# A float32 attention and gated feed-forward kernel: high and low parts interleaved row by row, sums by four transfers, statistics and value stores moved

## The chip, the cores and the metric

The kernel runs on one core of a Trainium2 chip. The metric is the device time of one execution in microseconds (us). PE is TensorE, DVE is VectorE, ACT is ScalarE, POOL is GpSimd; SP (SyncE) does nothing here but issue DMA transfers. DRAM is the chip's memory, SBUF the memory that the engines work from, in 128 partitions (rows), and PSUM the banks that PE writes its products to.

## The reference

```python
def reference(A_x, A_wqkv, A_wo, B_x, B_w1, B_w3, B_w2):
    x = A_x                                   # 1 x 2048 x 512, float32
    xn = layernorm(x, eps=1e-5)
    qkv = xn @ wqkv                           # 32 heads of 16
    p = softmax(q @ k.T * 16 ** -0.5)         # per head, 2048 x 2048
    s = (p @ v) @ wo
    g = silu((silu(xn @ w1) * (xn @ w3)) @ w2)   # inner width 1792
    return x + s * g
```

## The kernel before

**Exact products.** Each float32 operand is split into a high part, rounded to the format in which PE multiplies at full speed, and a low part, the rest. A product is then three: low by high, high by low, high by high (`split3`, `three`).

**Heads.** A head has 16 columns, so the three products of a score fit into one matmul with a contraction of 48 rows: the keys tile `ks` holds, per head, 48 rows made of high and low parts, and the queries tile `qs` the matching ones; further rows of `qs` carry the negative maxima of the scores (`mh`, `ml`), against rows of ones in `ks`. Two heads lie at partitions 0 and 64. The parts are made in the prologue, four blocks of 512 tokens at a time, stored to the DRAM tensors `qk` (`keep_rows`, L625), and loaded back as rows of a head (`load_k`, `load_q`). The helper `rows_in` does this with two transfers for each head: a merged one that brings both parts, 32 rows (L396), and one that brings one of the parts again, 16 rows (L398). In `qk` all 128 rows of one part lie together, then those of the other, so the merged transfer's source is 2 by 16 by columns.

**Order.** The kernel works in 32 half pairs (16 pairs of heads, two halves of 1024 queries). For each, maxima of scores are found first (matmul L422, DVE reduction L424), then scores again (L710), exponentials on ACT (L713), and products with the values (L726), whose 17th column of ones gives the sums. The matmuls of the feed-forward part (L1026) are woven in between. The order is written by hand in `ORDER_OF_ISSUE`; a small time model in the kernel only decides when side work, DMA issues among it, is put into the program. Each engine works through its own list in order. Nearly all DMA is issued by SP, in one list.

**The prologue** (to about 110 us) is ordered by the table `plan`: each row names a block's keys ("k"), queries ("q") or a tile's values ("v"), the tiles that are normalised and transposed next, the number of maxima to be done early, the number of token pieces to be stored to `xt` (L632), and further steps. `spread` computes a tile's mean and variance on DVE (three instructions) and two small POOL instructions; `norm` applies them on ACT. Values are copied by ACT into `vrow` (L560) and stored to DRAM `v` by DMAs that ACT issues (L566).

**Taking out a half pair** (`take_out`): the product is copied from PSUM to `ot`; the four rows of sums are brought to a 128 x 16 tile `sums` by one transfer (L737), inverted, stored to DRAM `rd` (L741), broadcast to all rows of `rb` by one transfer (L743), and multiplied on POOL (L745). This is done for 29 of the 32 half pairs; the last three take another way.

Semaphores: a transfer waits at its issuer until the one that used the same of eight slots before it has landed, whichever engine issued that one.

Of the kernel before, what the change touches and what calls it, by code (L numbers as in the profile page):

```python
# [9 lines left out]
F32 = mybir.dt.float32  # L10
F32R = mybir.dt.float32r
# [6 lines left out]
P = 128  # L18
S, D, F = 2048, 512, 1792
H, DH = 32, 16  # L20
NP = H // 2
KC = D // P
NT = S // P
TB = 4
# [3 lines left out]
VW = DH + 1  # L28
# [118 lines left out]
def raw(ap):  # L147
    return ap.bitcast(F32)
# [3 lines left out]
def kernel(ctx: ExitStack, tc: tile.TileContext, x, wqkv, wo, w1, w3, w2, out):  # L152
    nc = tc.nc
# [5 lines left out]
    dram = ctx.enter_context(tc.tile_pool(name="dram", bufs=1, space=DRAM))  # L159
# [18 lines left out]
    def bank(v):  # L178
        return take(v)[1]
# [2 lines left out]


    xt_d = [[dram.tile([P, KC * 512], F32R, name=f"xt{b}{s}") for s in range(2)] for b in range(TB)]
    qk_d = [dram.tile([2, P, S], F32R, name=f"qk{b}") for b in range(8)]
    o_d = [[dram.tile([P, 2, 512], F32R, name=f"o{b}{t}") for t in range(TB)] for b in range(KC)]
    v_d = dram.tile([NT, P, H * VW], F32, name="v")
    g_d = [dram.tile([512, D], F32, name=f"g{b}") for b in range(TB)]
# [19 lines left out]
    def run(gen):  # L208
        for _ in gen:
            pass  # L210
# [105 lines left out]
    class Weights:  # L316
# [47 lines left out]
    wts = Weights()  # L364
# [24 lines left out]
    def load_v(g):  # L389
        nc.sync.dma_start(room_v(g), v_d[:, :, g * GH * VW:(g + 1) * GH * VW].rearrange("t p (h d) -> p t h d", h=GH))  # L390

    def rows_in(t, two, src, r, h, cols):

        both = raw(src)[:, r:r + DH, cols]
        at = 64 * h + two * DH
        nc.sync.dma_start(raw(t)[at:at + 2 * DH, cols], both)  # L396
        at = 64 * h + 2 * (1 - two) * DH
        nc.sync.dma_start(raw(t)[at:at + DH, cols], both[1 - two])  # L398

    def load_k(p, cols=slice(0, S)):  # L400
        for h in range(2):
            rows_in(ks[p % 2], 0, qk_d[4 + p // 4], (p % 4) * 32 + h * DH, h, cols)

    def load_q(p, half, c=None):
        for h in range(2):
            rows_in(qs[p % 2], 1, qk_d[p // 4], (p % 4) * 32 + h * DH, h, c or slice(half * 1024, (half + 1) * 1024))

    def part_of(rbk, s):

        return raw(qk_d[rbk])[s if rbk < KC else 1 - s]  # L410

    mp, landed = {}, {}

# [38 lines left out]
    with tc.tile_pool(name="pro", bufs=1) as pro, tc.tile_pool(name="pros", bufs=1) as pros:  # L452
# [39 lines left out]
        def spread(t):  # L492

            st = pro.tile([P, 6], F32, tag="st", name="st", bufs=3)
            nc.vector.bn_stats(st, xin[t])
            mv = pro.tile([P, 2], F32, tag="mv", name="mv", bufs=6)
            nc.vector.bn_aggr(mv, st)
            ve = pro.tile([P, 1], F32, tag="ve", name="ve", bufs=3)
            nc.vector.tensor_scalar_add(ve, mv[:, 1:2], EPS)
            rs = pro.tile([P, 1], F32, tag="rs", name="rs", bufs=6)  # L500
            nc.gpsimd.tensor_tensor(rs, ve, minus, op=ALU.pow)
            nb = None
            if t > 0:
                nb = pro.tile([P, 1], F32, tag="nb", name="nb", bufs=6)
# [38 lines left out]
        def token_values(b, i):  # L543
            hi, lo = xts[b]
            ps = bank("m")
            three = [(h, k) for k in range(KC) for h in range(3)]
            if b == i == 0:

                three.sort(key=lambda e: ((2, 0, 1).index(e[0]), e[1]))
            elif b == 0:  # L550

                three.sort(key=lambda e: (e[0] == 0, e[1]))
            for n, (h, k) in enumerate(three):
                lhs = (lo, hi, hi)[h][:, k, i * P:(i + 1) * P]
                nc.tensor.matmul(ps, lhs, wv[k][h == 1], start=n == 0, stop=n == len(three) - 1)  # L555
# [4 lines left out]
            nc.scalar.copy(vrow[t % 4][:, :, 0:DH], v)  # L560
            nc.scalar.copy(vt[0][:, t, :, 0:DH], v[:, 0:GH, :])
            if b:
                store_values(t)

        def store_values(t):
            nc.scalar.dma_start(v_d[t], vrow[t % 4].rearrange("p h d -> p (h d)"))  # L566

        nc.gpsimd.memset(raw(ks[0]), 1.0)
        blank = iter([(raw(t), 0.0) for t in qs] + [(raw(ks[1]), 1.0)])
        spread(0)  # L570
        norm(0)
        split_w(0)
# [4 lines left out]
        split_w(2)  # L577
        split_w(3, nc.gpsimd)
        norm(1)
        vrow = [pros.tile([P, H, VW], F32, name=f"vrow{i}") for i in range(4)]  # L580
# [48 lines left out]
        def keep_tokens(n):  # L629
            for _ in range(n):  # L630
                b, s, k = next(stored_tokens)
                nc.sync.dma_start(raw(xt_d[b][s])[:, k * 512:(k + 1) * 512], raw(xts[b][s])[:, k, :])  # L632

        def more_tokens(n):

            transposed(n, xn.pop(n))
            if n + 2 < NT:
                norm(n + 2)
            if n + 4 < NT:
                spread(n + 4)  # L640

        def cols(b):
            return slice(b * 512, (b + 1) * 512)
# [1 line left out]
        def keys_here(b):  # L645
            return lambda: keep_rows(b, 1), lambda: load_k(0, cols(b))
# [8 lines left out]
            wts.pump(KC)  # L655
            wts.fill()

        def values_first():
            for t in range(TB):
                store_values(t)  # L660

        plan = [
            ("k", 0, (4, 5), 0, 0, keys_here(0)),
            ("q", 0, (6,), 0, 0, (values_first,)),
            ("v", 0, (7,), 0, 0, queries_here(0)),
            ("v", 1, (8,), 0, 1, ()),
            ("k", 1, (9, 10), 0, 2, ()),
            ("q", 1, (11,), 4, 2, keys_here(1)),
            ("v", 2, (12, 13), 5, 2, queries_here(1)),
# [4 lines left out]
            ("k", 3, (), 6, 1, (lambda: load_q(1, 0),)),  # L674
            ("q", 3, (), 6, 2, keys_here(3)),
            ("v", 1, (), 5, 2, queries_here(3) + (lambda: load_q(0, 1),)),
            ("v", 2, (), 6, 2, (blank_next, wts.start)),
# [4 lines left out]
            ("v", 3, (), 0, 0, ()),  # L682
        ]
        done = 0
        for what, n, tiles_, maxima_, pieces_, then in plan:
            if what == "v":
                run(token_values(1 + done // TB, n))
                done += 1
            else:
                token_rows(n, int(what == "k"))  # L690
            for _ in range(maxima_):
                max_unit(*next(early))
            for t in tiles_:
                more_tokens(t)
            for e in then:
                e()
            keep_tokens(pieces_)

    ring = ctx.enter_context(tc.tile_pool(name="ring", bufs=1))
# [29 lines left out]
    def take_out(p, half):  # L729

        ot = work.tile([P, 512], F32, tag="ot", name="ot", bufs=2)
        nc.scalar.copy(ot, pv)
        yield
        sums = work.tile([P, 16], F32, tag="sums", name="sums", bufs=2)
        rec = work.tile([P, 16], F32, tag="rec", name="rec", bufs=2)
        rd = dram.tile([4, 512], F32, name=f"rd{p * 2 + half}")
        nc.sync.dma_start(sums, ot[DH:P:32, :])  # L737
# [5 lines left out]
        nc.sync.dma_start(rb, rd.rearrange("j (o c) -> j o c", o=1).to_broadcast([4, 32, 512]))  # L743
# [307 lines left out]
    ov, wos, side, sums, there = {}, [], {}, {}, {}  # L1051
# [230 lines left out]
    for g in range(KC - 1):  # L1282
        p = 4 * g + 3
# [147 lines left out]
    for c in ORDER_OF_ISSUE:  # L1431
# [19 lines left out]
        elif c != "R":  # L1451
            what = (c.lower(), int(c.isupper()))
# [14 lines left out]
    ot, oh, ol = pt_tile(F32), pt_tile(F32R), pt_tile(F32R)  # L1467
# [20 lines left out]
    for t in range(4):  # L1488
        i, ps = take("o")
# [30 lines left out]
```

## Time and profile before

| | |
|---|---|
| Median of 3 runs | 1735.78 us (1734.87 to 1738.62) |
| Profiled execution | 1731.0 us, of which the span from first to last instruction 1729.2 |
| PE busy | 1698.3 us (98%) |
| DVE, ACT, POOL busy | 79%, 71%, 51% |
| Mean granted clock of PE | 0.995 |
| DMA moved | 184.81 MB, mean 107 GB/s |
| Merged loads (L396), 16-row loads (L398) | 104 each |

The profile's rows name a line, an engine, an operation and tiles as output<-input, with buffer numbers left out. "DMA ks<-qk" is a transfer's way from its issue to its landing, "SPq" is SP's time of issuing. In the chain of waits each row is a start and a length; in the timeline, the idle time before an instruction stands in brackets, with the name of what ended it by the profile. In windows, the last three columns are granted clock of PE (1.00 is full), busy share of the 16 DMA engines, and GB/s. A wait for several things is named after the last of them by the profile, so a name can be wrong where that engine had long been done.

### The profile page before, as it was taken

Reading aid. Unit: us, or ns where it says so; the run is one execution under the profiler, and the core shown is the slowest. Engines: PE = TensorE matmul, PEld = TensorE weight load, DVE = VectorE, ACT = ScalarE, POOL = GpSimd, SP = SyncE. Lnnn points to the kernel's source line nnn. Section 1 sums busy time; section 2 is a strip of 40 time slices with the busy share of each in tenths; the row PEclk is TensorE's granted clock in tenths of the full one; section 3 lists DMA queues with packets and bytes.
Section 4 is the critical chain, followed back from the end, with each engine's and each line's share of the span. In section 5 each row is a group of like instructions: output and inputs, shape, how many; then the busy total and the mean of one; then the engine's idle time right before and its main releaser. Section 6 shows DMA issues by size and latency. Waiting matters only on the chain.

```text
span 1729.2 us, 35378 instructions
## 1 busy us (share of the span) xinstructions
PE 1698.3 (98%) x13476; PEld 1128.3 (65%) x13476; DVE 1370.7 (79%) x2288; ACT 1230.9 (71%) x2449; POOL 878.9 (51%) x925
## 2 busy tenths in 40 slices
PE   9889999999998999999999999999999999999998
PEld 7566676666665767656666666766676666665466
DVE  5768988887886878788888778887887887888735
ACT  5237777778675777777777777777787777777852
POOL 5545553466544664366546663566456715753001
PEclk9989999999999999999999999999999999999999
DMA  6563433333234334142244424232332312331254
GB/s 230 190 205 113 134 106 86 96 112 93 78 112 133 107 102 120 56 109 54 72 131 141 132 83 128 75 90 60 98 100 75 81 38 71 92 108 35 77 176 175
DMA packets 164897, 184.81 MB, mean 107 GB/s; under 512 B 35640, under 2 KB 107320, under 8 KB 162520
## 3 DMA queue, kind: packets, MB, share of 16 engines
q1 hardware_dynamic: 161528, 176.52, 34.8%
q10 hardware_dynamic: 3200, 6.04, 0.9%
q8 instruction: 106, 1.74, 0.4%
q14 instruction: 63, 0.52, 0.1%
HBM read 135.36 MB, written 46.11 MB: 105 GB/s over the span
## 4 chain that ended last, share of the span: by engine, by line
PE 89%; DMA 5%; issue 2%; SPq 1%; POOL 1%; DVE 1%; ACT 1%; ACTq 0%; POOLq 0%; DVEq 0%
PE f L1026 31%; PE pv L726 26%; PE m L422 15%; PE e L710 15%; PE m L555 1%; DMA ks<-qk 1%; DMA qk<-sl 1%; DMA qs<-qk 1%; SPq L396 1%; DMA inh<-in_A_x_dram 1%; PE o L201 0%; PE m L437 0%; DMA ovh<-o 0%; PE o L203 0%; PE o L205 0%
## 5 line engine op out<-in xcount | busy, mean ns | idle before, releaser
L424 DVE TENSOR_REDUCE mp<-m 128x1 f32<-128x512 f32 x2048 | 1277.2, 683 | 242.9 <-PE m L422 170.9
L713 ACT ACTIVATE pt<-e 128x512 f32<-128x512 f32 x2048 | 1058.6, 611 | 270.9 <-PE m L422 134.4
L422 PE MATMUL m<-ks,qs 62*128 62x512 f32 x2048 | 744.7, 413 | 19.8 <-ACT g L849 8.2
L710 PE MATMUL e<-qs,ks 64*128 64x512 f32 x2048 | 742.2, 407 | 1.3 <-DMA qs<-ml 1.3
L726 PE MATMUL pv<-pt,vt 128*17 128x512 f32 x4096 | 480.1, 596 | 0.0
L422 PEld LDWEIGHTS m<-ks,qs 62*128 62x128 f32 x2048 | 352.0, 185 | 130.3 <-issue 38.2
L710 PEld LDWEIGHTS e<-qs,ks 64*128 64x128 f32 x2048 | 352.2, 184 | 105.9 <-issue 35.4
L726 PEld LDWEIGHTS pv<-pt,vt 128*17 128x17 f32 x4096 | 100.8, 97 | 253.9 <-issue 249.3
L1026 PE MATMUL f<-xtl,wh 64*128 64x512 f32 x504 | 184.0, 391 | 0.0
L1026 PE MATMUL f<-xth,wh 64*128 64x512 f32 x504 | 181.3, 392 | 0.0
L1026 PE MATMUL f<-xth,wl 64*128 64x512 f32 x504 | 181.1, 392 | 0.0
L1026 PE MATMUL f<-wh,hs 64*128 64x512 f32 x528 | 167.1, 393 | 0.0
L1026 PE MATMUL f<-xtl,xeh 64*128 64x512 f32 x440 | 161.0, 391 | 0.0
L1026 PE MATMUL f<-xth,xeh 64*128 64x512 f32 x440 | 158.4, 392 | 0.0
L1026 PE MATMUL f<-xth,xel 64*128 64x512 f32 x440 | 157.5, 395 | 0.0
L869 POOL TENSOR_TENSOR h<-g,h 128x512 f32<-128x512 f32 x56 | 72.1, 1288 | 163.1 <-ACT h L865 163.0
L340 POOL TENSOR_TENSOR wl<-wr,wh 128x512 fp32r<-128x512 f32 x105 | 135.5, 1290 | 8.8
L1026 PE MATMUL f<-xeh,hs 64*128 64x512 f32 x368 | 118.7, 394 | 0.4 <-POOL hs L871 0.4
L340 POOL TENSOR_TENSOR xel<-wr,xeh 128x512 fp32r<-128x512 f32 x87 | 112.3, 1290 | 7.3
L339 POOL TENSOR_SCALAR xeh<-wr 128x512 fp32r<-128x512 f32 x87 | 54.1, 621 | 120.3 <-PE m L422 56.1
L1026 PE MATMUL f<-wl,hs 64*128 64x512 f32 x264 | 99.0, 392 | 0.0
L339 POOL TENSOR_SCALAR wh<-wr 128x512 fp32r<-128x512 f32 x105 | 65.3, 622 | 63.6 <-PE e L710 42.1
(242 smaller groups left out, 2166.6 us busy)
## 6 DMA issues: line engine op xcount, KB each, us to landing
wr<-in_B_w_dram SPq DMA_DIRECT2D x168, 256.0 KB
ovh<-xt SPq DMA_DIRECT2D x36, 256.0 KB
ovl<-xt SPq DMA_DIRECT2D x36, 256.0 KB
qs<-qk SPq DMA_DIRECT2D x62, 128.0 KB
wr<-in_A_wqkv_dram SPq DMA_DIRECT2D x30, 256.0 KB
ks<-qk SPq DMA_DIRECT2D x30, 256.0 KB
o<-o SPq DMA_DIRECT2D x120, 64.0 KB
rb<-rd SPq DMA_DIRECT2D x29, 256.0 KB
```

Of the source, the lines that this page charges most:

```text
L339: nc.gpsimd.tensor_scalar(hi, t, 1.0, 1.0, op0=ALU.mult, op1=ALU.mult)
L340: nc.gpsimd.tensor_sub(lo, t, raw(hi))
L396: nc.sync.dma_start(raw(t)[at:at + 2 * DH, cols], both)
L422: nc.tensor.matmul(ps, qs[p % 2][64 * h:64 * h + KM, q0:q0 + P], ks[p % 2][64 * h:64 * h + KM, c * 512:(c + 1) * 512], start=True, stop=True)
L424: nc.vector.reduce_max(mp[p, half][:, h, qt, c:c + 1], ps, axis=AX.X)
L555: nc.tensor.matmul(ps, lhs, wv[k][h == 1], start=n == 0, stop=n == len(three) - 1)
L710: nc.tensor.matmul(ps, ks[p % 2][64 * h:64 * h + KR, k * P:(k + 1) * P], qs[p % 2][64 * h:64 * h + KR, q0:q0 + 512], start=True, stop=True)
L713: done = nc.scalar.activation(pt, ps, AF.Exp, scale=DH ** -0.5)
L726: nc.tensor.matmul(pv[32 * j:32 * j + VW, :], vt[2 * p // GH][:, key, 2 * p % GH + j % 2, :], pt, start=key < 2 if last else k == 0, stop= ...
L869: nc.gpsimd.tensor_mul(h2, g, h2)
L1026: nc.tensor.matmul(ps, left[r], right[r], start=starts and lane == 0, stop=ends and lane == 1)
```

## The change

1. `qk` in DRAM becomes rows by parts: the high and the low part of a row lie next to each other. The merged transfer is then 32 rows of one stride; rows of `ks` and `qs` interleave the parts, and the third sixteen rows repeat the high part for both.
2. The one transfer of sums becomes four, one for each row of sums; the one broadcast becomes four of 16 rows each, to the rows that hold products. The rows of `rb` between are set to 1 once.
3. Statistics of tiles 8 to 15 are computed two tiles at a time beside tiles 4 to 7 of the transposes; before, one tile beside each of tiles 4 to 11. Their small tiles get a buffer each.
4. Value stores go from ACT's list to SP's and are gathered: `keep_values(n)` stores what has been made until n remain. `vrow` has six buffers instead of four. Token pieces are spread a little differently over the plan.

```diff
-    qk_d = [dram.tile([2, P, S], F32R, name=f"qk{b}") for b in range(8)]
+    qk_d = [dram.tile([P, 2, S], F32R, name=f"qk{b}") for b in range(8)]
...
-        both = raw(src)[:, r:r + DH, cols]
-        at = 64 * h + two * DH
-        nc.sync.dma_start(raw(t)[at:at + 2 * DH, cols], both)
-        at = 64 * h + 2 * (1 - two) * DH
-        nc.sync.dma_start(raw(t)[at:at + DH, cols], both[1 - two])
+        both = raw(src)[r:r + DH, :, cols]
+        nc.sync.dma_start(raw(t)[64 * h:64 * h + 2 * DH, cols], both.rearrange("r s c -> (r s) c"))
+        nc.sync.dma_start(raw(t)[64 * h + 2 * DH:64 * h + 3 * DH, cols], both[:, high, :])
...
-        return raw(qk_d[rbk])[s if rbk < KC else 1 - s]
+        return raw(qk_d[rbk])[:, s if rbk < KC else 1 - s, :]
...
-            nc.scalar.copy(vrow[t % 4][:, :, 0:DH], v)
+            nc.scalar.copy(vrow[t % 6][:, :, 0:DH], v)
             nc.scalar.copy(vt[0][:, t, :, 0:DH], v[:, 0:GH, :])
-            if b:
-                store_values(t)
-
-        def store_values(t):
-            nc.scalar.dma_start(v_d[t], vrow[t % 4].rearrange("p h d -> p (h d)"))
+            made_values.append(t)
+
+        made_values = []
+
+        def keep_values(left):
+            while len(made_values) > left:
+                t = made_values.pop(0)
+                nc.sync.dma_start(v_d[t], vrow[t % 6].rearrange("p h d -> p (h d)"))
...
-        blank = iter([(raw(t), 0.0) for t in qs] + [(raw(ks[1]), 1.0)])
+        blank = iter([(raw(t), 0.0) for t in qs] + [(r, 1.0) for r in (raw(ks[1]), rb)])
...
-            if n + 4 < NT:
-                spread(n + 4)
+            for i in range(2 * n, min(2 * n + 2, NT)):
+                spread(i)
...
-            ("q", 0, (6,), 0, 0, (values_first,)),
+            ("q", 0, (6,), 0, 0, ()),
             ("v", 0, (7,), 0, 0, queries_here(0)),
-            ("v", 1, (8,), 0, 1, ()),
+            ("v", 1, (8,), 0, 0, ()),
...
+            if done > 1:
+                keep_values(int(what == "v"))
             keep_tokens(pieces_)
...
-        nc.sync.dma_start(sums, ot[DH:P:32, :])
+        for j in range(4):
+            nc.sync.dma_start(sums[32 * j:32 * j + 32, :], ot[32 * j + DH:32 * j + VW, :])
...
-        nc.sync.dma_start(rb, rd.rearrange("j (o c) -> j o c", o=1).to_broadcast([4, 32, 512]))
+        for j in range(4):
+            nc.sync.dma_start(rb[32 * j:32 * j + DH, :], rd[j:j + 1, :].to_broadcast([DH, 512]))
```

What moves in the lists: PE's list is the same in both, instruction by instruction. On SP in the prologue, from the loads of the first block's queries to the loads of the second block's keys, there stood before (`sh` and `sl` are the high and low part on their way to `qk`, `xt00<-xeh` a piece of tokens):

```order
L396 DMA qs0_108<-qk0_74 32x1x512
L398 DMA qs0_108<-qk0_74 16x512
L632 DMA xt00_66<-xeh_214 128x512 x3
L625 DMA qk4_78<-sh_615 128x512
L625 DMA qk4_78<-sl_616 128x512
L396 DMA ks0_110<-qk4_78 32x1x512
L398 DMA ks0_110<-qk4_78 16x512
```

and there stands now, lines being numbered a little differently (L395 is the merged load, L396 the 16-row one):

```order
L395 DMA qs0_108<-qk0_74 32x512
L396 DMA qs0_108<-qk0_74 16x512
L567 DMA v_98<-vrow0_235 128x544
L567 DMA v_98<-vrow1_236 128x544
L567 DMA v_98<-vrow2_237 128x544
L567 DMA v_98<-vrow3_238 128x544
L567 DMA v_98<-vrow4_239 128x544
L567 DMA v_98<-vrow5_240 128x544
L633 DMA xt00_66<-xeh_214 128x512 x2
L626 DMA qk4_78<-sh_647 128x512
L626 DMA qk4_78<-sl_648 128x512
L395 DMA ks0_110<-qk4_78 32x512
```

Six value stores have come in between, and one piece of tokens has moved behind the keys. On ACT, these stores stood before ahead of the copy of the next values and the high part of the next tile (`xth`):

```order
L616 COPY sc_498<-e_483 128x512
L526 CAST xth_437<-m_502 128x4x128
L514 ACTIVATE xn_509<-xin8_273,nb_456,rs_454 128x512
L566 DMA v_98<-vrow0_235 128x544
L566 DMA v_98<-vrow1_236 128x544
L566 DMA v_98<-vrow2_237 128x544
L566 DMA v_98<-vrow3_238 128x544
L560 COPY vrow0_235<-m_525 128x32x16
L561 COPY vt_243<-m_525 128x4x16
L566 DMA v_98<-vrow0_235 128x544
L526 CAST xth_437<-m_541 128x4x128
```

and now ACT's list runs through:

```order
L617 COPY sc_522<-e_507 128x512
L524 CAST xth_441<-m_526 128x4x128
L512 ACTIVATE xn_533<-xin8_277,nb_460,rs_458 128x512
L558 COPY vrow4_239<-m_555 128x32x16
L559 COPY vt_247<-m_555 128x4x16
L524 CAST xth_441<-m_570 128x4x128
```

On DVE, between one low part (`xtl`) and the next, there stand now the statistics of two tiles, where there was one:

```order
L525 TENSOR_TENSOR xtl_442<-m_472,xth_441 128x4x128
L493 BN_STATS st_481<-xin10_327 128x6
L495 BN_AGGR mv_483<-st_481 128x2
L497 TENSOR_SCALAR ve_485<-mv_483 128x1
L493 BN_STATS st_491<-xin11_329 128x6
L495 BN_AGGR mv_493<-st_491 128x2
L497 TENSOR_SCALAR ve_495<-mv_493 128x1
L525 TENSOR_TENSOR xtl_442<-m_526,xth_441 128x4x128
```

The small POOL steps of these statistics have moved with them, ahead of the splits of the next keys and queries.

More of the change, by code (lines that the diff above doesn't have):

```diff
@@ L390, in load_v, with rows_in @@
         nc.sync.dma_start(room_v(g), v_d[:, :, g * GH * VW:(g + 1) * GH * VW].rearrange("t p (h d) -> p t h d", h=GH))
-    def rows_in(t, two, src, r, h, cols):
-        both = raw(src)[:, r:r + DH, cols]
-        at = 64 * h + two * DH
-        nc.sync.dma_start(raw(t)[at:at + 2 * DH, cols], both)
-        at = 64 * h + 2 * (1 - two) * DH
-        nc.sync.dma_start(raw(t)[at:at + DH, cols], both[1 - two])
+    def rows_in(t, high, src, r, h, cols):
+        both = raw(src)[r:r + DH, :, cols]
+        nc.sync.dma_start(raw(t)[64 * h:64 * h + 2 * DH, cols], both.rearrange("r s c -> (r s) c"))
+        nc.sync.dma_start(raw(t)[64 * h + 2 * DH:64 * h + 3 * DH, cols], both[:, high, :])
     def load_k(p, cols=slice(0, S)):
         for h in range(2):
-            rows_in(ks[p % 2], 0, qk_d[4 + p // 4], (p % 4) * 32 + h * DH, h, cols)
+            rows_in(ks[p % 2], 1, qk_d[4 + p // 4], (p % 4) * 32 + h * DH, h, cols)
     def load_q(p, half, c=None):
         for h in range(2):
-            rows_in(qs[p % 2], 1, qk_d[p // 4], (p % 4) * 32 + h * DH, h, c or slice(half * 1024, (half + 1) * 1024))
+            rows_in(qs[p % 2], 0, qk_d[p // 4], (p % 4) * 32 + h * DH, h, c or slice(half * 1024, (half + 1) * 1024))
     def part_of(rbk, s):
-        return raw(qk_d[rbk])[s if rbk < KC else 1 - s]
+        return raw(qk_d[rbk])[:, s if rbk < KC else 1 - s, :]
     mp, landed = {}, {}
@@ L495, in spread @@
             nc.vector.bn_stats(st, xin[t])
-            mv = pro.tile([P, 2], F32, tag="mv", name="mv", bufs=6)
+            mv = pro.tile([P, 2], F32, tag="mv", name="mv", bufs=NT)
             nc.vector.bn_aggr(mv, st)
@@ L499, in spread @@
             nc.vector.tensor_scalar_add(ve, mv[:, 1:2], EPS)
-            rs = pro.tile([P, 1], F32, tag="rs", name="rs", bufs=6)
+            rs = pro.tile([P, 1], F32, tag="rs", name="rs", bufs=NT)
             nc.gpsimd.tensor_tensor(rs, ve, minus, op=ALU.pow)
@@ L503, in spread @@
             if t > 0:
-                nb = pro.tile([P, 1], F32, tag="nb", name="nb", bufs=6)
+                nb = pro.tile([P, 1], F32, tag="nb", name="nb", bufs=NT)
                 nc.gpsimd.tensor_scalar(nb, mv[:, 0:1], rs, -1.0, op0=ALU.mult, op1=ALU.mult)
@@ L579 @@
         norm(1)
-        vrow = [pros.tile([P, H, VW], F32, name=f"vrow{i}") for i in range(4)]
+        vrow = [pros.tile([P, H, VW], F32, name=f"vrow{i}") for i in range(6)]
         for v in vrow:
@@ L656, in weights_first @@
             wts.fill()
-        def values_first():
-            for t in range(TB):
-                store_values(t)
         plan = [
             ("k", 0, (4, 5), 0, 0, keys_here(0)),
-            ("q", 0, (6,), 0, 0, (values_first,)),
+            ("q", 0, (6,), 0, 0, ()),
             ("v", 0, (7,), 0, 0, queries_here(0)),
-            ("v", 1, (8,), 0, 1, ()),
+            ("v", 1, (8,), 0, 0, ()),
             ("k", 1, (9, 10), 0, 2, ()),
@@ L673 @@
             ("v", 0, (), 6, 2, (blank_next,)),
-            ("k", 3, (), 6, 1, (lambda: load_q(1, 0),)),
+            ("k", 3, (), 6, 2, (lambda: load_q(1, 0),)),
             ("q", 3, (), 6, 2, keys_here(3)),
             ("v", 1, (), 5, 2, queries_here(3) + (lambda: load_q(0, 1),)),
-            ("v", 2, (), 6, 2, (blank_next, wts.start)),
+            ("v", 2, (), 6, 2, (blank_next, blank_next, wts.start)),
             ("v", 3, (), 6, 2, (weights_first,)),
@@ L681 @@
             ("v", 2, (), 0, 0, ()),
-            ("v", 3, (), 0, 0, ()),
+            ("v", 3, (), 0, 0, (lambda: keep_values(0),)),
         ]
```

## The prediction

> **What bounds the kernel now.** I read the page first, then who PE waits for, then the chain of waits around each of those waits, then DMA by the microsecond.
>
> ```profile
> span 1729.2 us, 35378 instructions
> PE 1698.3 (98%) x13476; PEld 1128.3 (65%) x13476; DVE 1370.7 (79%) x2288; ACT 1230.9 (71%) x2449; POOL 878.9 (51%) x925
> ```
>
> PE is the bound: 31 us of the span are not PE work. The change leaves PE's list in the same order, so it can only win or lose waits, and what the clock does after them. Two answers on PE's waits, one for 0 to 125 us and one for 150 to 1700 us (total, times, longest):
>
> ```profile
> PE m L422 <- DMA ks<-qk: 6.7, 2, 5.5
> PE e L710 <- DMA qs<-ml: 1.3, 1, 1.3
> ...
> PE m L422 <- ACT g L849: 8.2, 3, 5.6
> PE m L422 <- DMA ks<-qk: 0.9, 1, 0.9
> ```
>
> Nearly all stand around a load of keys or queries. The timeline places them (start, length, in brackets the idle time before), and the chain tells what ran meanwhile (start, length):
>
> ```profile
> 46.56 0.73 PE L422 MATMUL m<-ks,qs 62*128 62x512 f32 x4
> 49.48 0.47 PE L422 MATMUL m<-ks,qs 62*128 62x512 f32 x1 [2.19 <-DVE mp L424]
> ...
> 60.51 0.50 PE L422 MATMUL m<-ks,qs 62*128 62x512 f32 x2 [1.87 <-DMA qs<-qk]
> 89.10 0.76 PE L422 MATMUL m<-ks,qs 62*128 62x512 f32 x1 [5.54 <-DMA ks<-qk]
> 90.97 1.62 PE L422 MATMUL m<-ks,qs 62*128 62x512 f32 x5 [1.11 <-DMA ks<-qk]
> ...
> 538.14 0.79 PE L422 MATMUL m<-ks,qs 62*128 62x512 f32 x1 [5.57 <-ACT g L849]
> ```
>
> ```profile
> 26.42 2.44 DMA qk<-sl
> ...
> 42.27 3.17 DMA qk<-sl
> 45.49 3.67 DMA ks<-qk
> 68.70 3.08 DVE mp L424 x5
> 77.63 7.26 DMA qk<-sl
> 86.72 4.11 DMA ks<-qk
> 92.59 4.71 PE m L555 x12
> 98.20 2.96 PE m L555 x12
> 108.26 4.01 DMA qs<-ml
> ...
> 516.55 7.57 SPq L396
> 524.99 9.80 DMA qs<-qk
> ```
>
> The reader is to see: a 256 KB store lands in 2.44 us in a quiet moment and in up to 7.26 us elsewhere; a 64 KB load takes 3.67 us; one load at 525 us takes 9.80 us after SP had hung 7.57 us on issuing another. The wait at 49.48 is named after DVE, but keys of block 1 landed at 45.49 + 3.67 = 49.16, and these are what that product first needs: I count it as a wait for keys. The one at 538.14 is the same at one remove: SP was late, so a store from a buffer that ACT wanted back was late. Why are the transfers slow? DMA share and GB/s are the last two columns:
>
> ```profile
> 44.00:45.00 1.00, 1.00 (x6) 0.82 (x5) 1.00 (x3) 1.00 (x2) 0.90 (x3) 1.00 0.13 49
> 50.00:51.00 1.00, 1.00 (x9) 1.00 (x10) 0.68 (x1) 0.43 (x1) 0.00 (x0) 1.00 1.04 385
> 520.00:521.00 1.00, 1.00 (x14) 0.52 (x8) 0.17 (x2) 0.04 (x1) 0.92 (x3) 1.00 0.12 49
> ```
>
> DMA can do 385 GB/s, yet right when PE is about to starve it does 49, on 0.12 of sixteen engines: two of them. What is under way then is the merged load of L396, whose source has the two parts, high and low, as its first dimension. Everything that lies behind it on those two engines is late too, a 128-row store for instance, since it has a share on each.
>
> The Trainium skill (DMA: Bandwidth & Descriptors, "Why a DMA increments its semaphore by 16 and not by 1") says that a transfer is given the largest number of engines up to 16 that divides the slowest dimension above 1 of both sides. By that rule the old merged load gets 2 engines and the new one, with 32 rows first, 16; the trace agrees for the old one (0.12 of 16).
>
> **The change part by part.**
>
> *Merged loads.* 32 rows of one stride instead of 2 by 16. Bounds for the new landing: above, today's 3.67 us; below, the 2.44 us of the quiet 256 KB store, which moves more bytes with 128 rows. I take the lower one: the load of one head pair and block, 192 KB, is 0.5 us at 385 GB/s. SP also issues it faster, if it becomes like its 16-row neighbour (ns, min/median/max):
>
> ```profile
> L396 SPq DMA_DIRECT2D qs<-qk x66: 600/622/7572, 37.0 to 1520.1; - x66
> L398 SPq DMA_DIRECT2D qs<-qk x66: 302/410/1161, 37.7 to 1525.3; - x66
> L737 SPq DMA_DIRECT2D sums<-ot x29: 594/611/2935, 169.3 to 1562.5; - x29
> L743 SPq DMA_DIRECT2D rb<-rd x29: 552/592/605, 192.3 to 1576.0; - x29
> ```
>
> That is 0.21 us for each of 104 (66 of queries, 38 of keys).
>
> *Value stores and statistics.* Today ACT issues the stores, and hangs while their slots come free (the name after the idle 4.59 us is that of a keys load, but the four instructions ahead of it are stores):
>
> ```profile
> 33.73 0.59 ACT L560 COPY vrow<-m 128x512 f32<-128x512 f32 x1 [4.59 <-DMA ks<-qk]
> 35.36 0.49 PE L201 MATMUL e<-xth,wkl 128*128 128x512 f32 x1 [1.12 <-ACT xth L526]
> 36.08 0.50 PE L203 MATMUL e<-xtl,wkh 128*128 128x512 f32 x1 [0.23 <-DVE xtl L527]
> ```
>
> Without that ACT is free at 33.73 - 4.59 = 29.1, and PE's two waits, 1.35 us, go. Statistics of two tiles instead of one now stand between two low parts on DVE; they cost what these rows say, and POOL has two more small steps ahead of its next split:
>
> ```profile
> 25.44 0.68 DVE L495 BATCH_NORM_STATS2 st<-xin 128x6 f32<-128x512 f32 x1
> 26.52 0.68 DVE L527 TENSOR_TENSOR xtl<-m,xth 128x512 fp32r<-128x512 f32 x1
> ```
>
> 26.52 - 25.44 = 1.08 us a tile on DVE. From 25.44 on, three low parts (0.6 each) and six tiles end by about 33.8, when PE (35.36 less its 1.12, 34.2) wants the last low part: covered, by 0.4 us. If that cover fails, PE loses a few tenths.
>
> What moves to SP is dearer: six stores of 272 KB plus two of 256 KB now lie, on SP's one queue, between the queries' load and the store of keys block 1. With that store (512 KB) they are 2.7 MB, 7.0 us at 385 GB/s.
>
> ```profile
> 38.80 0.41 SPq L398 DMA_DIRECT2D qs<-qk  x1
> ```
>
> The queries' last load was issued by 38.80 + 0.41 = 39.2; I have it at 37.7 (two merged loads of keys and two of queries, 0.21 less each, and some 0.7 for slots that come free sooner, an estimate). So data flows from about 38.2 to 45.2, has landed at 45.8 (today 45.44); the first head's two loads are issued by 46.7, and by 2 us of landing, a little under the quiet 2.44, its keys are there near 48.7. PE arrives at 47.29 - 1.35 = 45.9 and waits 2.8 us instead of 2.19. It goes on at 48.7 instead of 49.48: **0.8 us won** (bounds: 3.5 if all 1.35 + 2.19 went; -5 if the queue ran at the mean 211 GB/s of the next row instead of 385).
>
> ```profile
> 40.00:50.00 10.00, 7.81 (x38) 5.21 (x37) 9.48 (x21) 4.52 (x9) 6.44 (x11) 1.00 0.58 211
> 84.00:100.00 16.00, 9.79 (x32) 6.71 (x33) 6.00 (x10) 0.99 (x4) 0.00 (x0) 0.68 0.51 164
> 530.00:560.00 30.00, 24.43 (x181) 12.63 (x180) 16.11 (x29) 13.94 (x29) 16.71 (x18) 0.89 0.59 153
> ```
>
> *Queries block 1.* The keys' loads are issued by 47.6; two token stores and the queries' store, 1 MB, are then 2.7 us of queue and landed at 51.5, the load by 55. PE gets there at 60.5 - 49.5 = 11 us after the keys today, 1.9 of them idle, so at 48.7 + 9.1 = 57.8. **1.9 us won** (0 to 1.9).
>
> *Keys block 3.* By the same steps the keys of block 2 are issued near 61.5. Between them and this store lie 3.7 MB (four pairs of tokens, the queries' store, two values, next queries), 10 us of queue, then its own 512 KB: landed at 74, loaded at 77.5. PE is there at 89.10 - 5.54 - 2.7 = 80.9. Margin 3.4 us. So 5.54 + 1.11 go, and with them the slow clock: the mean of 0.68 over 84 to 100 us is (1 - 0.68)/0.5 x 16 = 10.2 us at half clock, in which twelve products took 4.71 instead of 2.96 us, five 1.62 instead of about 0.8 (four took 0.73 at 46.56), one some 0.3 more: 2.8 us. **9.45 us won** (0 to 9.45). Late next is DVE, with six maxima of 3.08/5 = 0.62 us, 3.7 us, for PE's twelve products and six maxima, 2.96 + 0.9 us: just fast enough.
>
> *First rows of maxima.* Their load took 4.01 us behind value stores; with 2.44 it would be early. But SP's half stands behind the last token and value stores. **1.0 us won** (0 to 1.3).
>
> *Main loop.* The wait at 538.14 and its clock: 0.89 over 530 to 560 is (1 - 0.89)/0.5 x 30 = 6.6 us at half clock, which would be 3.3 us lost had PE worked all through; it stood still for part of it, and I take 2.6; 5.57 + 2.6 = **8.2 us won** (0 to 8.2). The 0.9 us for keys at 924 us goes too: **0.9 us**. The other 2.6 us named after ACT I leave.
>
> *Sums and broadcast in four.* Four transfers of about 0.41 us for one of 0.61, and four for one of 0.59: 3.28 - 1.20 = 2.1 us more on SP in each of 29 half pairs, 60 us; the merged loads give back 104 x 0.21 = 22 us. SP does this beside PE, as it waits for others most of the time:
>
> ```profile
> SPq L449 <- ACT mh L440: 199.1, 31, 18.1
> ```
>
> The broadcast brings half the bytes, and rows of rb that are no longer brought are set once, 0.5 us on POOL. I take 0 (bounds: +1.3 and -10; see below).
>
> Sum: 0.8 + 1.9 + 9.45 + 1.0 + 8.2 + 0.9 = 22.3 us. The profiled execution took 1731.0 us (span 1729.2), 4.8 below the median of the runs, 1735.8. Its successor should take 1708.7, and the median be 1735.8 - 22.3 = **1713.5 us**.
>
> **The rivals.**
>
> *The value stores starve keys block 1.* At 211 GB/s the 2.7 MB take 12.8 us, PE waits 8.6 instead of 2.8 and the clock falls, as it did in both long waits: 5.8 + 2.7 less: 1722. For it: that mean was real in just this stage. Against: two starved engines are in it.
>
> The skill's TensorE: Matmul & The Clock Gate, "Part 1: The HAM clock gate", puts the idle window that halves the clock at about 3.4 us. By that rule my own 2.8 us would be safe or nearly so; the trace agrees with it in that 2.19 us left the clock at 1.00 and 5.5 us did not.
>
> *All waits for DMA and behind it go,* the 2.6 us under ACT's name and my 2.8 us too: 1708.
>
> *Transfers stay on two engines,* so the change doesn't do what it says: only the 1.35 us on ACT go, 1734.5. Against: the 128-row stores reach 1.04.
>
> *Slower: SP's queue becomes late for the rows of maxima.* Each half pair PE needs four small row loads that SP issues in turn. SP spends (60 - 22)/29 = 1.3 us more per half pair, plus slots it waits for. Once SP issues them after ACT has them ready, and not before, each microsecond is PE's: with 2.1 us in each of 29, 61 - 22 = 39 us, 1775; in half of them, 1744. Against: SP waits 199 us for ACT at just that place.
>
> **How the numbers follow.** Forecast 0.60 (its own range 1708 to 1718); starved keys 0.16; all waits 0.08; two engines 0.08; SP late 0.08. The range, 1705 to 1726, holds the first three but some of the second's upper end, 0.83. A difference of 0.2% (3.5 us) is what a measurement can tell. Faster: 0.60 + 0.15 + 0.08 + 0.02 = 0.85; same 0.08; slower 0.07.
>
> **What would show it.** Right: no hang on the merged load's issue above 1 us and a median near 410 ns; no stretch of 0.12 at 49 GB/s behind a merged load; PE's wait near 85 and 535 us gone, clock at 1.00 there; a wait of 2 to 3.5 us for keys near 46. Wrong: that wait above 5 us with a clock of 0.5, or new waits for qs<-ml all through the main loop.

## The result, and the profile after

The changed kernel takes 1705.7 us in the median of four runs (1704.52 to 1705.91). The kernel before, run on the same chip beside it, takes 1736.3 (1734.87 to 1738.62). The ratio is 0.9821, with a 95% interval from 0.9804 to 0.9838. The gain is 30.6 us where 22.3 were forecast. The median lies 7.8 us under the forecast of 1713.5: inside the wide range, by 0.7 us of its lower end, and outside the forecast's own range of 1708 to 1718. The profiled execution took 1704.5 us.

The page of the changed kernel (busy time and share of the span):

```profile
span 1702.7 us, 35617 instructions
PE 1691.6 (99%) x13476; PEld 1126.6 (66%) x13476; DVE 1370.3 (80%) x2288; ACT 1230.6 (72%) x2449; POOL 879.8 (52%) x928
```

The span is 26.5 us shorter. PE's busy time fell by 6.7 us with the same 13476 products. PE worked 11.5 us at half clock before and 3.4 now, which explains 4.1 of these; the other 2.6 stay open. The remaining 19.8 us of the span were idle time. PE's waits from 0 to 125 us, and behind the dots from 150 to 1700 us, are (total, times, longest):

```profile
PE m L420 <- DMA ks<-qk: 3.0, 1, 3.0
PE pv L485 <- POOL minus L480: 1.4, 1, 1.4
...
PE f L1027 <- POOL hs L872: 0.4, 1, 0.4
PE o L201 <- DVE pt L1487: 0.3, 1, 0.3
```

Lines are numbered a little differently: L420 is what L422 was. One wait for keys is left, and the main loop has none. The three waits named "ACT g" (8.2 us) are gone with those for keys. The timeline has the one that is left:

```profile
48.57 0.74 PE L420 MATMUL m<-ks,qs 62*128 62x512 f32 x1 [3.05 <-DMA ks<-qk]
```

The chain of waits ahead of it (start, length):

```profile
42.77 3.38 DMA qk<-sl
...
46.20 0.32 SPq L395
...
46.57 1.87 DMA ks<-qk
```

The row of 1.87 us is the first head's 16-row load, issued behind the merged one. The merged load itself, which took 3.67 us, landed 1.91 us after its issue by the trace of its semaphore, the counter that tells of a landing. Windows show why, and what the wait did to the clock (last three columns: granted clock, DMA share, GB/s):

```profile
40.00:41.00 1.00, 1.00 (x6) 0.59 (x6) 0.22 (x1) 0.30 (x2) 0.00 (x0) 1.00 1.04 405
...
43.00:44.00 1.00, 1.00 (x5) 0.77 (x5) 1.00 (x3) 0.40 (x1) 0.59 (x1) 1.00 1.02 373
...
47.00:48.00 1.00, 0.00 (x0) 0.00 (x0) 0.80 (x2) 0.00 (x0) 0.00 (x0) 1.00 0.38 98
...
50.00:51.00 1.00, 1.00 (x7) 1.00 (x5) 0.04 (x1) 0.61 (x2) 0.00 (x0) 0.50 1.02 385
...
84.00:100.00 16.00, 16.00 (x77) 11.78 (x77) 9.39 (x17) 4.05 (x13) 7.56 (x8) 1.00 0.74 241
530.00:560.00 30.00, 30.00 (x258) 20.29 (x258) 24.45 (x41) 22.21 (x44) 21.53 (x22) 1.00 0.30 71
```

Of the span's windows of 1 us, 86 had a share of 0.11 to 0.13 at 44 to 54 GB/s before; 3 have now, none of them behind a merged load. Up to 45 us the stores run on all sixteen engines. From 47 to 48 us only loads of keys are under way (the next piece of tokens is issued at 47.95), and the share is 0.38 where four such loads on the same two engines could not pass 0.12. In the two long windows, where the clock was 0.68 and 0.89, PE is busy all through at full clock. But for the last 2 us of the span, the clock is halved only from about 48.6 to 52.0 us, behind the wait of 3.05 us. SP's rows (ns, min/median/max) and its longest wait:

```profile
L395 SPq DMA_DIRECT2D qs<-qk x66: 302/418/1283, 35.6 to 1495.1; - x66
...
L737 SPq DMA_DIRECT2D sums<-ot x116: 502/584/1372, 154.5 to 1538.1; - x116
...
L744 SPq DMA_DIRECT2D rb<-rd x116: 317/418/2093, 177.5 to 1551.1; - x116
...
SPq L447 <- ACT mh L438: 207.5, 31, 18.7
```

The merged load is issued in 0.42 us instead of 0.62, and its worst case, once 7.6 us, is 1.3. Sums and broadcast cost SP 4 x (0.584 + 0.418) = 4.0 us for 1.2 before, so 2.8 us more in each half pair. SP still waits over 200 us for ACT at the rows of maxima.

PE's list is the same in all kernels, so one can ask when the same product starts. Time won by then, in us, against the profiled execution of before (left: the start there; "again" is a second profile of before; the others are the experiments below):

```
start   again  sums   values  layout  layout+  change  change,
before         alone  alone   alone   sums             early stores
 38.1    0.2    0.0    2.2     2.0     2.0      1.8     2.0
 49.5   -1.3   -1.6   -3.7     4.4     4.4      0.9     3.9
 52.9   -2.8   -3.1   -5.2     4.5     4.5     -0.6     3.9
 61.9   -2.1   -2.2   -4.8     6.3     6.3      1.5     5.9
 98.1   -2.3   -1.0   -4.7    14.8    14.8     11.4    14.6
125.0   -1.6   -1.0   -4.6    15.5    14.9     13.1    15.7
200.0   -6.1   -3.1  -11.6    17.1    16.6     14.8    17.4
529.9   -6.1   -3.3  -11.9    16.9    16.3     14.8    17.2
545.1   -6.2   -4.2  -11.4    25.5    24.7     23.3    25.8
800.0   -5.2   -3.7  -10.2    27.6    26.5     25.3    28.0
935.9   -4.9   -7.4  -10.2    28.7    26.3     26.3    29.1
1722.9  -6.3   -9.8  -10.8    28.8    26.0     26.2    29.2
```

### The profile page after: what moved, and what is told of

It reads as the page before. It is cut to its first block, busy times and chain, and to the rows that moved or that the text cites. A ratio compares the mean times of both kernels' runs of the same rounds, so it can differ in the third digit from the quotient of the medians.

```text
span 1702.7 us, 35617 instructions
## 1 busy us (share of the span) xinstructions
PE 1691.6 (99%) x13476; PEld 1126.6 (66%) x13476; DVE 1370.3 (80%) x2288; ACT 1230.6 (72%) x2449; POOL 879.8 (52%) x928
## 4 chain that ended last, share of the span: by engine, by line
PE 95%; DMA 2%; issue 2%; SPq 1%; POOL 1%; DVE 0%; ACT 0%; ACTq 0%; POOLq 0%; DVEq 0%
PE f L1027 32%; PE pv L725 26%; PE m L420 16%; PE e L709 15%; PE m L553 2%; PE e L201 0%; DMA ovl<-o 0%; PE m L520 0%; PE e L203 0%; PE e L205 0%; PE m L435 0%; DMA inl<-g 0%; DMA inh<-in_A_x_dram 0%; DMA wr<-in_A_wqkv_dram 0%; SPq L762 0%
## 5 line engine op out<-in xcount | busy, mean ns | idle before, releaser
L422 DVE TENSOR_REDUCE mp<-m 128x1 f32<-128x512 f32 x2048 | 1276.7, 683 | 223.9 <-PE m L420 142.7
L420 PE MATMUL m<-ks,qs 62*128 62x512 f32 x2048 | 741.9, 412 | 3.0 <-DMA ks<-qk 3.0
L420 PEld LDWEIGHTS m<-ks,qs 62*128 62x128 f32 x2048 | 351.0, 184 | 110.7 <-issue 32.4
L941 POOL TENSOR_SCALAR th<-th 128x512 f32<-128x512 f32 x16 | 9.9, 621 | 169.6 <-ACT th L937 169.6
```

The source lines that it names most:

```text
L420: nc.tensor.matmul(ps, qs[p % 2][64 * h:64 * h + KM, q0:q0 + P], ks[p % 2][64 * h:64 * h + KM, c * 512:(c + 1) * 512], start=True, stop=True)
L422: nc.vector.reduce_max(mp[p, half][:, h, qt, c:c + 1], ps, axis=AX.X)
L941: nc.gpsimd.tensor_scalar(th, th, 1.0, 1.0, op0=ALU.add, op1=ALU.mult)
```

## The experiments

### Which part carries the gain

Theory: the merged load on all engines carries nearly all. Rival: the move of the value stores has its own share, through ACT. Each part was built alone.

The layout alone (part 1: `qk` and the loads as in the change; sums, statistics and value stores as before):

> The kernel before with the row-by-row layout of high and low parts alone (part 1). Theory (two engines): the merged loads are what all large waits of PE stood behind, so nearly the whole gain is here. Gone: 1.9 us at 60 us, 9.5 to 10 at 89, 1.3 at 112, 8.6 at 538, 0.9 at 934, and the 2.6 us under ACT's name; the 1.35 us behind ACT's stores at 35 us stays, the wait for keys at 49 falls to about 0.3. Median near 1711 (1708 to 1716). Rival (value stores and statistics were the cause): 1733 or more.

Measured: 1702.9 us (1702.2 to 1706.1); before beside it 1733.5 (1731.9 to 1739.1, nine runs); ratio 0.9825 [0.9803, 0.9847]. PE's waits:

```profile
PE pv L485 <- POOL minus L480: 1.4, 1, 1.4
PE m L420 <- DVE mp L422: 0.8, 1, 0.8
PE e L708 <- DMA qs<-ml: 0.7, 1, 0.7
```

The layout alone is as fast as the whole change, 8 us faster than expected, and no wait for keys is left. It also removes PE's wait at 35 us, though ACT still issues the value stores: 2.0 us are won by 38 us. Values alone win 2.2 there. Either edit takes ACT's hang away, so the two gains don't add.

Sums and broadcast by four transfers alone (part 2, with the old loads), and statistics and value stores alone (part 3, that is points 3 and 4 of the change, with the old loads):

> The kernel before with sums and broadcast by four transfers alone (part 2). Theory: SP's 2 us more per half pair are hidden, and no wait of PE goes: 1736 (1734 to 1739), with the long waits near 85 and 535 us still there. Rival (the one-transfer sums and broadcast held up SP's queue and with it the queries' load at 538): 8 to 12 us faster, 1726.

> The kernel before with value stores on SP and statistics two by two alone (part 3). Theory: the 1.35 us at 35 us go, but value stores and two-engine loads then share SP's queue, so the waits for keys of blocks 1 and 3 stay or grow: 1736 (1731 to 1744). Rival (stores on ACT's queue took the bandwidth of the keys): 12 us faster, 1724.

Measured: 1740.6 us (1739.9 to 1743.8), ratio 1.0038 [1.0024, 1.0052], and 1742.1 (1741.2 to 1743.4), ratio 1.0045 [1.0028, 1.0063]. Alone, both parts make the kernel slower, by 7.1 and 8.5 us; for the sums that is more than the expected range allowed. PE's waits with sums alone:

```profile
PE m L422 <- DMA ks<-qk: 13.3, 5, 5.0
PE m L422 <- ACT g L851: 8.0, 2, 7.4
```

and the chain with values alone:

```profile
43.43 0.67 SPq L628
...
44.20 4.94 DMA qk<-sl
```

With the loads on two engines the store of keys block 1 lands in 4.94 us behind the value stores; in the change it took 3.38 behind the same six. For the sums, the prologue is as late at 53 us (3.1) as that of the second profile of before (2.8), ahead of any such transfer. Further on, rows tie a part of the loss to the new transfers: four of them stand on SP ahead of a load of keys, for which PE then waits 3.10 us (0.9 in the first profile of before):

```profile
925.29 2.46 SPq L738 DMA_DIRECT2D sums<-ot  x4
...
929.45 0.69 SPq L396 DMA_DIRECT2D ks<-qk  x1
```

```profile
939.70 0.76 PE L422 MATMUL m<-ks,qs 62*128 62x512 f32 x1 [3.10 <-DMA ks<-qk]
```

Before, the one transfer took SP 0.62 us there. From 800 to 936 us sums alone lose 3.7 us in the table, and the second profile of before loses none. Where the rest of the 7.1 us goes stays open.

The second profile of before:

> The kernel before, unchanged, for a second profile. The first profiled execution took 1731.0 us, 5 us less than the median of its runs. Theory (with loads on two engines, what lies ahead of them differs a little from run to run): its waits at the same places differ from those of the first profile by some us in all, in the prologue above all. Rival (the profiled execution is simply shorter): the waits agree within 0.5 us each.

One run: 1737.4 us, 6.3 above the profiled execution that the prediction used. Its waits:

```profile
PE m L422 <- DMA ks<-qk: 12.9, 5, 4.9
PE m L422 <- ACT g L849: 5.9, 2, 5.5
```

The same program waits differently from run to run: the first profile had 7.5 us for keys, 2.2 more that I count as such under DVE's name, and 8.2 under ACT's.

### Parts 2 and 3 with the new loads

The change without part 2, and the layout with part 2 but without part 3:

```diff
-        for j in range(4):
-            nc.sync.dma_start(sums[32 * j:32 * j + 32, :], ot[32 * j + DH:32 * j + VW, :])
+        nc.sync.dma_start(sums, ot[DH:P:32, :])
...
```

> The changed kernel with sums and broadcast back in one transfer each (parts 1 and 3 without part 2). Theory (part 2 only hurts where loads on two engines make slots scarce): as the changed kernel, 1705.5 within 1.5. Rival (six more transfers per half pair cost slots still): 4 us or more below the changed kernel, 1701.

> Layout and sums by four without moving value stores and statistics (parts 1 and 2). Theory (part 3 is what costs the changed kernel its wait for keys of block 1): as the layout alone, 1703 within 1.5, no wait for keys near 46 us above 1 us. Rival (part 2 costs as much as it did with the old layout, 7 us): 1709.

Measured: 1705.4 us (1705.3 to 1706.4), ratio 0.983 [0.9815, 0.9844], and 1704.6 (1703.5 to 1704.9), ratio 0.9823 [0.9808, 0.9837]. With the new loads part 2 is worth nothing that can be told: 1705.4 without and 1705.7 with it beside part 3, and 1702.9 without and 1704.6 with it beside the layout alone, in ranges that overlap. The table of starts puts 1.3 us of that last difference between 800 and 936 us, in one profile each. There the layout with sums has a wait behind the same four transfers of sums, 2.49 us on SP, and the layout alone has none:

```profile
907.46 0.47 PE L420 MATMUL m<-ks,qs 62*128 62x512 f32 x1 [1.12 <-DMA ks<-qk]
```

The change, with the same four transfers ahead of that load, has no such wait.

The table also shows what part 3 does: at 38 us the change is 0.2 us behind the layout alone, at 49.5 us 3.5. The timeline of the change has SP's list in that stretch:

```profile
37.43 3.17 SPq L567 DMA_DIRECT2D v<-vrow  x6
40.66 1.32 SPq L633 DMA_DIRECT2D xt<-xeh  x2
42.08 0.59 SPq L626 DMA_DIRECT2D qk<-sh  x1
42.77 0.65 SPq L626 DMA_DIRECT2D qk<-sl  x1
```

POOL had the high part ready at 38.5 us, but six value stores stood ahead of its store. So four of them were sent before the queries:

```diff
+        keep_values(0)        # right after the values of the first block, ahead of the queries' steps
```

> The changed kernel with the stores of the first four value tiles issued as soon as these are made (near 20 us, when DMA is nearly idle) instead of behind the loads of the first queries. Theory (1.1 MB of value stores ahead of the store of keys block 1 make the wait of 3.05 us and the half clock after it): the wait falls to 0.5 or less, no half clock; 3.5 to 4.5 us below the changed kernel, 1701.5. Rival (value stores on SP's list cost wherever they stand, through slots): 1705 or more.

> The last one without part 2: layout, values on SP with the first four early, statistics two by two, sums and broadcast in one transfer each. Theory: no wait of PE for DMA above 1 us is left, 1701 within 1.5, the same as the layout alone or 1 to 2 us less. Rival (part 2 costs slots): 4 us below the one with part 2.

Measured: 1700.6 us (1700.2 to 1701.6) with part 2, ratio 0.9802 [0.9787, 0.9816], and 1701.2 (1700.7 to 1701.9) without it, ratio 0.9805 [0.9788, 0.9822]. On this same chip the change without part 2 took 1705.4: the early stores are worth 4.2 us, in ranges that don't meet. The timeline of SP, with early stores:

```profile
37.26 0.84 SPq L567 DMA_DIRECT2D v<-vrow  x2
38.15 0.96 SPq L634 DMA_DIRECT2D xt<-xeh  x2
39.20 0.55 SPq L627 DMA_DIRECT2D qk<-sh  x1
39.85 0.56 SPq L627 DMA_DIRECT2D qk<-sl  x1
```

and its chain:

```profile
39.85 3.40 DMA qk<-sl
...
43.67 1.83 DMA ks<-qk
```

The store goes out 2.9 us earlier and takes as long (3.40). PE's long wait goes, and the half clock with it. This is the best version of all: 5 us under the change.

### Is it the engines, or the shape?

Rival to "all engines": the source's two rows lying next to each other, or one stride, makes the load fast. The old layout without the two-part dimension, as two loads of 16 rows each:

```diff
-        nc.sync.dma_start(raw(t)[at:at + 2 * DH, cols], both)
+        for s in range(2):
+            at = 64 * h + (two + s) * DH
+            nc.sync.dma_start(raw(t)[at:at + DH, cols], both[s])
```

> The kernel before with its old layout; each merged load of 2 by 16 rows is issued as two plain loads of 16 rows, so a head is brought by three transfers of 16 rows. Theory (what counts is on how many engines a load runs, not how the rows lie in DRAM): as the layout alone, within 3 us of it, about 1711, though SP issues 104 transfers more (0.2 us each net, hidden). Rival (the layout itself, longer runs of rows, makes it faster): no gain, 1736.

The new layout alone, its 32 rows issued as 16 and 16, or as 31 and 1:

```diff
-        nc.sync.dma_start(raw(t)[64 * h:64 * h + 2 * DH, cols], both.rearrange("r s c -> (r s) c"))
+        rows = both.rearrange("r s c -> (r s) c")
+        for a, b in ((0, 16), (16, 2 * DH)):        # the other kernel: ((0, 31), (31, 2 * DH))
+            nc.sync.dma_start(raw(t)[64 * h + a:64 * h + b, cols], rows[a:b, :])
```

> The layout alone, with the merged load of 32 rows issued as two of 16 rows: three transfers a head, as in the run with three plain loads, but in the new layout. Theory (what the run with three loads lost against the layout alone, 11 us, is the price of 104 more transfers, which hold slots): 1714 within 3. Rival (it lost them by the old layout in DRAM): 1703.

> As the last one, but the 32 rows are issued as 31 and 1: the same number of transfers and bytes, the same layout. Theory (a load gets the largest number of engines up to 16 that divides its rows, 31 rows one engine): a load of 31 rows then runs at some 25 GB/s, 2.5 us of engine time for a block and 10 us for a whole pair of keys, worse than the kernel before: long waits for keys and queries all along, 1745 or more. Rival (it is the number of transfers and SP's time that count, not engines): 1714.

Measured: 1714.2 us (1713.9 to 1715.3), ratio 0.9885 [0.9868, 0.9902], for the old layout in three loads; 1719.0 (1718.2 to 1719.5), ratio 0.9911 [0.9891, 0.993], for 16 and 16; 1869.3 (1867.3 to 1873.6), ratio 1.0782 [1.0757, 1.0807], for 31 and 1. The last two issue the same number of transfers and move the same bytes from the same layout; one is 150 us slower. The chain of the 31-row kernel, and a window of it while that load runs:

```profile
28.87 6.74 DMA ks<-qk
```

```profile
33.00:34.00 1.00, 1.00 (x6) 0.75 (x5) 0.00 (x0) 0.00 (x0) 0.00 (x0) 1.00 0.06 25
```

That is 0.06 of sixteen: one engine, 25 GB/s, half of what the old load got on two. The semaphores say the same: in the traces each of the 104 old merged loads moves its counter in 3 steps, each 31-row load in 2, and each 32-row or 16-row load in 16. So the number of engines decides; layout and stride are only a way to get a first dimension that sixteen divides. The rule that the Trainium skill gives (DMA: Bandwidth & Descriptors, "Why a DMA increments its semaphore by 16 and not by 1") asks for 2 engines for the old shape, 16 for 32 rows and 1 for 31. The traces agree: 0.12 and 0.06 for the first and the last, and for the one between 0.38 with nothing else under way, 1.91 us where it was 3.67, and the 16 steps.

But two 16-row loads, also on sixteen engines, are 11 to 16 us dearer than one of 32, where the first run was expected within 3 us of the layout alone and the second at 1714 within 3. The chain of the kernel with 16 and 16 showed a possible cause:

```profile
80.97 2.15 DMA v<-vrow
...
83.14 0.30 SPq L397
...
83.48 1.96 DMA ks<-qk
```

SP couldn't issue the keys until a value store, which ACT had issued late, had landed: slots are shared, and more transfers reach them sooner. Theory: this is the cost. Rival: more transfers cost by themselves. With early stores all value stores are in SP's list, and so that cannot happen; 16 and 16 was put into that kernel.

> The kernel after with early value stores (all four of the first block straight away, all value stores on SP), but the 32-row loads issued as 16 and 16 rows: the same 104 more transfers that cost the layout alone 16 us (1718.96 against 1702.91). In that kernel the row of the chain at 80.97 us shows a value store that ACT had issued, 2.15 us, and SP's next load of keys issued only when it had landed. Theory: the 16 us come from value stores that ACT issues late and that hold slots which the loads on SP need; with every value store on SP, in one list with the loads, that cannot lie across the list in this way, so 1701 to 1706 us and no half clock near 85 us. Rival: more transfers cost by themselves, 18 more in the prologue of 0.4 us each on SP and as many slots: 1711 to 1719, with waits for keys near 82 to 86 us as before.

Measured: 1711.4 us (1710.3 to 1713.0), ratio 0.9866 [0.9844, 0.9888]: 10.8 us above the same kernel with 32 rows, as the rival said. The theory fell for most of it: 10.8 of the 16 us are left. The waits for keys are still there, and so is the half clock behind them, from 84.9 to 88.3 us (84.6 to 91.4 with 16 and 16 in the layout alone):

```profile
82.47 0.47 PE L422 MATMUL m<-ks,qs 62*128 62x512 f32 x1 [1.62 <-DMA ks<-qk]
83.93 0.93 PE L422 MATMUL m<-ks,qs 62*128 62x512 f32 x5 [0.98 <-DMA ks<-qk]
```

```profile
85.00:86.00 1.00, 1.00 (x3) 0.82 (x4) 1.00 (x3) 0.00 (x0) 0.00 (x0) 0.50 1.00 377
```

The chain says where the loss comes from:

```profile
79.65 0.32 SPq L397
...
80.02 0.41 SPq L397
...
80.48 0.42 SPq L398
```

SP's own issuing is on the path ahead of PE's wait for the second head's keys. The prologue has 18 more transfers of about 0.42 us each, 7.6 us of SP's list, and by PE's starts 9.5 us of the loss are there by 125 us. That the rest comes from slots wasn't separated, nor the 5 us between 1714.2 and 1719.0.

## Why the prediction was right, and where it was wrong

Terms of the sum beside what the table's finer form shows for the change:

| Term | forecast | measured |
|---|---|---|
| Keys block 1, with ACT's hang | 0.8 | 0.9 |
| Clock after that wait | 0 | -1.6 |
| Queries block 1 | 1.9 | 2.1 |
| Keys block 3 and half clock | 9.45 | 9.9 |
| First rows of maxima | 1.0 | 1.75 |
| Wait at 538 us and clock | 8.2 | 8.6 |
| Keys at 924 us | 0.9 | 1.1 |
| The other waits under ACT's name (152, 742 us) | 0 | 3.7 |
| Sums and broadcast | 0 | 0 by the medians |
| Sum in the profile | 22.3 | 26.5, after small drifts |

**Engines.** Right, and shown: two engines set the time of the merged loads, and held up what lay behind them.

**Keys block 1.** Right to a few tenths. DMA ran at 373 to 405 GB/s from 39 to 45 us; the step had 385 from 38.2 to 45.2. The store landed at 46.15 (forecast 45.8), the load at 48.4 (48.7), PE waited 3.05 us (2.8). The rival of starved keys at 211 GB/s fell; that mean belonged to the two-engine loads, and values alone support it: with the old loads PE waited 4.66 us there.

**The clock behind it.** Wrong. The step took 2.8 us as nearly safe, because 2.19 us had left the clock at 1.00. It cost 1.6 us. Why the 2.19 us had left it is in the last section.

**Keys block 3, and the wait at 538.** Right; the margin was thinner than forecast, since the loads were issued at 77.7 us and not at 74. In the layout alone they went at 73.2.

**"The other 2.6 us named after ACT I leave."** Wrong: the largest missing term, 3.7 us. They are the same kind as the wait at 538, which the step did take; layout alone wins them (1.7 us by 152, 2.0 at 742), with ACT's work untouched. Why it is more than the 2.6 us of waits stays open.

**ACT's hang.** The 1.35 us went, but the step gave moving the stores as the cause. The layout alone does it too: the name in the row, a keys load that held a slot, was right, and the stores' place on ACT was only where it showed.

**Moving value stores.** The step saw what the move does to keys block 1, and priced it inside a gain of 0.8. Priced against the layout alone it is a loss of 5.1 us by 52.9 us, half clock included, of which half has come back by the end. The cover of 0.4 us for the statistics held: no wait for a low part shows.

**The rivals.** Two engines did not stay. SP was not late for the rows of maxima: the change has no wait for `qs<-ml` at all. Closest came "all waits go", 1708: the 2.6 us under ACT's name did go, and the wait of 2.8 us, which it let go too, stayed.

**Sums.** With the new loads the medians can't tell it from zero; the 1.1 us wait of layout with sums is the only row against it. SP's extra time was 81 us rather than 60. It is hidden, but not shown to be where the step put it: SP waits no less for ACT at the rows of maxima than before (207.5 us, 199.1 before). With the old loads part 2 was slower, which the step did not allow for.

**From profile to median.** Wrong by 3.6 us, nearly half of the miss. The step took the 4.8 us between before's profiled execution and its median as a constant. It is not: runs of before scatter from 1731.9 to 1739.1, those of the change over 1.4 us, and the change's profiled execution lies 1.2 below its median. The second profile of before shows its own extra 6.3 us at waits that the new loads shorten or remove.

## What to carry to other kernels

When DMA is slow while PE starves, read share and GB/s by the microsecond: 0.12 of sixteen names the number of engines, and the fix is a first dimension that sixteen divides, in as few transfers as before, since each further one is some 0.4 us of the issuer's list where that list is on the path. Put stores that nobody waits for ahead of the moment when that list becomes urgent, or behind it, not into it: four early stores were worth 4.2 us. Where the kernel before scatters between runs, the scatter is part of what a change can win, so subtract a gain from the profiled execution and ask which of the waits varies.

## What the runs showed of the hardware that was not expected

The same idle time does not always do the same to the clock. In the first profile of before PE idled 2.19 us and the next microseconds ran at 1.00. With sums alone, at the same product:

```profile
51.03 0.47 PE L422 MATMUL m<-ks,qs 62*128 62x512 f32 x1 [2.20 <-DMA ks<-qk]
```

A wait of 2.20 us was followed, a microsecond after it had ended, by the half clock. In the second profile of before one of 2.90 us did the same.

The profiles show where the difference lies. The granted clock changes only on a beat of 3.41 us. In the first profile of before it is 0.50 from 86.13 to 96.37 us and from 536.69 to 543.52, three and two beats, and 1.00 for 129 beats between. Counted back from 86.13, a beat ends at 48.59 us, within the wait of 2.19 us, which lasts from 47.29 to 49.48. The two beats that share it (the second figure is PE's busy time):

```profile
45.17:48.58 3.41, 2.12 (x11) 1.14 (x9) 3.27 (x8) 0.71 (x3) 2.11 (x3) 1.00 0.20 55
48.60:51.99 3.39, 2.51 (x15) 2.06 (x16) 2.05 (x4) 1.42 (x3) 0.66 (x2) 1.00 0.99 370
```

With sums alone one beat holds the whole wait; here it is, with the beat behind it:

```profile
48.46:51.86 3.40, 1.20 (x9) 0.62 (x6) 2.81 (x5) 0.44 (x2) 0.59 (x2) 1.00 0.66 238
51.87:55.26 3.39, 3.39 (x12) 2.91 (x11) 0.36 (x1) 2.48 (x4) 2.29 (x3) 0.50 0.58 210
```

Idle times of 1.3 and 0.9 us in two beats left the clock at 1.00; 2.2 us in one beat halved it in the next. In the change the beat from 45.19 to 48.60 us had 3.05. In all fourteen profiles, but for the first 5 and the last 20 us of each span, every beat at full clock with 1.9 us or more of idle time was followed by the half clock, and none with less than 1.3. That fits what the Trainium skill says of a window that runs freely (TensorE: Matmul & The Clock Gate, "Part 1: The HAM clock gate"), so that where a wait falls in it counts; but its about 3.4 us of idling was not needed in any of these. No run here varied the place alone: the beats compared are those of different kernels.
